# Attention, a gated layer and a rational layer in one kernel: the rational part's tile order, the place of the gated part's leftovers, and the shares of a weight conversion are changed

## The chip, the core and the metric

The program runs on one core of a Trainium2 chip. Its engines are TensorE (PE in the profile, with its weight loads as PEld), VectorE (DVE), ScalarE (ACT), GpSimd (POOL) and SyncE (SP), which here only issues transfers. The metric is the device time of one execution in microseconds, given as the median of several runs.

## The reference, cut to what matters

Local attention with a window of 32 and 32 global tokens per head, then a gated layer, then a layer with a rational function between its two products:

```python
# 4 batches x (512 local + 32 global) tokens = 2176 rows, 512 wide
out_g = softmax(q_g k_all^T / 8) v_all                       # 32 global queries see everything
out_l = softmax([q_l k_g^T, q_l k_l^T where |i-j| <= 32] / 8) [v_g, v_l]
x = concatenate([out_g, out_l])  ->  rows of 512
gate = 1 / (1 + exp(-(x @ w_gate)));  val = x @ w_val        # 512 -> 1536
x = (gate * val) @ w_out                                     # 1536 -> 512
h = x @ w_in                                                 # 512 -> 2048
P = a0 + a1 h + a2 h^2 + a3 h^3
Q = 1 + |b0| |h| + |b1| h^2
out = (P / (Q + 1e-6)) @ w_out2                              # 2048 -> 512
```

Every product is done in three: high part by high part, low by high, high by low. All inputs come as 64-bit words, of which a weight has to be rebuilt on the core (its "conversion").

## The kernel before, in words

The program is written in the order in which each engine is to run it; nothing reorders it later. A wait of one instruction therefore holds up all that is written behind it on the same engine, and on SP all transfers behind it.

**Attention** runs over 16 units (a batch and a pair of heads). Its steps are listed in `STEPS` with a number each, the place in units of progress; the list is sorted by these places and issued. `load` steps issue the transfers of q, k, v (`qn`, `kn`, `vn`, `wn`), `g_load` those of the global queries (`qgn`), which the products of line 303 (`pair<-kn,qgn`) read for every second unit. Between them stand the first weights: `w_raw` and `w_next` issue the transfer of one raw weight (`fetch`, lines 544 to 548, tile `raw`, three buffers), and `w_mag`, `w_bits`, `w_add`, `w_hi`, `w_lo` convert it: two ACTs (lines 564 and 565), two DVEs (572 and 573), a POOL addition (580), an ACT cast (602) and a POOL subtraction (610). Since there are three `raw` buffers, the transfer of weight number 5 waits until weight 1 has gone through line 573 (tile `v10gv`).

**The gated part** keeps the 2176 rows in five tiles: 0 to 3 of 512 local rows, and `GLOB` (4) of the 128 global rows. It goes through the 12 column blocks of w_gate and w_val in six pairs; in each pair tiles 0, 1 and GLOB are done: `first` (24 matmuls, gate and value, in banks of the pool `ps1`, which has three), a sigmoid on ACT (line 748, which frees the gate's bank), a product on DVE (749, which frees the value's bank), a cast and a subtraction, and `second`, two halves of 12 matmuls that DVE adds into `gacc`. Beside each pair runs a share of the conversions of later weights; `Pace` spreads them over the pair and `pace.finish()` issues what is left at its end. `AT_ONCE` says how many weights of the rational part are converted beside each pair, besides the pair's own six. A converted weight is written to DRAM (`keep`, line 594) and read back later (line 659). Behind the six pairs the sums of tiles 0 and 1 are split and sent to DRAM ("parked": lines 845 and 846, tiles `sty`), tile GLOB is turned back by `final_glob` (four transposes of line 810 into a `ps1` bank, a cast, a subtraction), and tiles 2 and 3 follow, from pair 1 on in a Strassen scheme that needs seven products of quarter size; the rest of the conversions run beside it. `back(i)` reads tile i from DRAM again, in eight transfers.

**The rational part** works in turns. A turn starts one unit: `first` (12 matmuls, line 710 to 712, or 719 to 721 for GLOB), and brings the earlier ones forward by one step each: on ACT `abs` (1150), `lin` (1153), `p3` (1161), `log` (1174), `exp` (1178), `hi` (1199); on DVE `p2` (1165), `r1` (1182), `p1` (1169), `r2` (1186), `quot` (1190); on POOL `quad` (1157) and `lo` (1211). Four turns later comes `second` (12 matmuls, lines 1240 to 1242). A GLOB unit has to be transposed on PE three turns after its start (line 1206, tile `rt`), right behind its `quot`. Within each of four groups the units come in the order `LAST_TURNS`. `rest(n)`, called at the end of turn n, issues what the gated part has left over: the last four halves of `second` (`queue`), the eight parks of tiles 2 and 3 (`parks`: a cast on ACT, line 845, and a subtraction, line 846, on DVE or POOL in turn), and `back(1)`.

Of the kernel before, what the change touches and what calls it, by code (L numbers as in the profile page):

```python
# [29 lines left out]
LN_SCALE = 2.0**-32  # L30

TILES = [(0, 512), (512, 512), (1024, 512), (1536, 512), (2048, 128)]
GLOB, LAST_TURNS = 4, (0, 4, 2, 1, 3)


def tile_of(tok):
# [76 lines left out]
    ('x_out', (397.6786, 9.48477, 15.22727, 12.74181, 508.4924, 477.88016)),  # L113
    ('w_raw', (5.02089, 6.82068, 0.49824, 10.1341)),
    ('w_next', 4, (14.0,)),
    ('w_next', 5, (14.1,)),
    ('w_next', 6, (41.0,)),
    ('w_mag', (5.27805, 7.32394, 4.37884, 25.24838)),
    ('w_bits', (5.94689, 13.87965, 5.77964, 40.08108)),
# [329 lines left out]
class Weights:  # L449
# [4 lines left out]


    EARLY, AHEAD = 4, 3
    AT_ONCE = (0, 1, 2, 1, 1, 5)
    RING2 = (4, 5, 6, 7, 0, 1, 2, 3, 8, 9, 10, 11)

    def __init__(self, tc, early, dram, ins, outs):  # L460
# [14 lines left out]
        for p, f in enumerate(range(2, NF + 1, 2)):  # L475
            m = n + self.AT_ONCE[p]
            if f < NF:
# [255 lines left out]
def gated(nc, pools, only, xpool, dram, wp, ident, xh, xl):  # L733
# [34 lines left out]
    def first(f, i):  # L768
        pg = pools.ps1.tile([128, 512], F32, tag="p1", name=f"pg{f}_{i}")
        pv = pools.ps1.tile([128, 512], F32, tag="p1", name=f"pv{f}_{i}")  # L770
        layer(nc, pg, wp, 1, f, "gate", xh[i], xl[i])
        layer(nc, pv, wp, 1, f, "val", xh[i], xl[i])
        return split(gate(pg, pv, f"{f}_{i}"), f"{f}_{i}")
# [31 lines left out]
    def final_glob():  # L805

        n = TILES[GLOB][1]
        ps = pools.ps1.tile([128, 512], F32, tag="p1", name="pty")
        for m in range(4):
            nc.tensor.transpose(ps[:, m * n : m * n + n], acc[GLOB][:, m], ident)  # L810
        yh[GLOB] = xpool.tile([128, 4, n], F32R, tag=f"xh{GLOB}", name=f"yh{GLOB}")
        yl[GLOB] = xpool.tile([128, 4, n], F32R, tag=f"xl{GLOB}", name=f"yl{GLOB}")
        src = ps.rearrange("p (m t) -> p m t", m=4)
        nc.scalar.copy(yh[GLOB], src)
        nc.vector.tensor_tensor(yl[GLOB], src, yh[GLOB].bitcast(F32), ALU.subtract)
# [54 lines left out]
    def put(i, k, x, eng):  # L870
        if not turned:
            t12h, t12l, t34h, t34l = (xpool.tile([128, 4, 512], F32R, tag=n, name=f"t{n}") for n in ("xh0", "xl0", "xh1", "xl1"))
            turned.extend([(t12h[:, 0:2], t12l[:, 0:2]), (t12h[:, 2:4], t12l[:, 2:4]),
                           (t34h[:, 0:2], t34l[:, 0:2]), (t34h[:, 2:4], t34l[:, 2:4])])
        src = held[x, k]
        h, l = (t[:, k] for t in turned[i])
        nc.scalar.copy(h, src)
        eng.tensor_tensor(l, src, h.bitcast(F32), ALU.subtract)
# [10 lines left out]
    def c1(k):  # L889
        held["a", k], held["b", k] = ztile(f"za{k}"), ztile(f"zb{k}")  # L890
        less((held["a", k], held["b", k]), at((0, 1), k), at((0, 0), k), nc.vector)
# [14 lines left out]
    def c3(k):  # L906
        held["d", k], held["e", k] = ztile(f"zd{k}"), ztile(f"ze{k}")
        less((held["d", k], held["e", k]), at((1, 1), k), at((0, 1), k), nc.gpsimd)
# [50 lines left out]
    def back(i):  # L959
        yh[i] = xpool.tile([128, 4, 512], F32R, tag=f"xh{i}", name=f"yh{i}")  # L960
        yl[i] = xpool.tile([128, 4, 512], F32R, tag=f"xl{i}", name=f"yl{i}")
        for m in range(4):
            t = wp.kept[9, i, "y", m]
            nc.sync.dma_start(yh[i][:, m].bitcast(F32), t[:, 0:512])
            nc.sync.dma_start(yl[i][:, m].bitcast(F32), t[:, 512:1024])
# [102 lines left out]
    park()  # L1068
    wp.allow(1)
    gs.append(first(1, 2))  # L1070
    final_glob()
    c1(1)
    park()
    c2(1)
# [5 lines left out]
    c4(1)  # L1080
    wp.allow(1)
    pending.pop(0)()
    put(1, 1, "b", nc.vector)
    c3(1)
    park()
# [19 lines left out]
    pace.finish()  # L1105

    def rest(n):
        for _ in range({1: 2, 2: 2}.get(n, 0)):
            queue.pop(0)()
        for _ in range({3: 4, 4: 2, 5: 2}.get(n, 0)):  # L1110
            parks.pop(0)()
        if n == 3:
            back(1)

    return yh, yl, rest

# [1 line left out]
def rational(nc, pools, rest, wp, ident, xh, xl, before, co, out):  # L1118
# [152 lines left out]
    for n in range(len(units) + 8):  # L1271
        if n == 1:
            nc.scalar.preload_act_table_set("natural_log_exp_and_others")
        for name, ahead, *args in PLAN2:
            u = n + ahead
            if name in ("second", "out") and u >= LATER:
                u -= 1
                if u < LATER:
                    continue
            if 0 <= u < len(units):  # L1280
                steps[name](u, *args)
                fs, i = units[u]
                if i == LAST_TURNS[-1] and name == "second":
                    wp.release((2, fs[0], "out", 0))
                if i == LAST_TURNS[-1] and name == "first" and fs[0] % G == G - 1:
                    for k in range(4):
                        wp.release((2, fs[0] - G + 1, "in", k))
        before(n)
        wp.pump(len(wp.loads))


@with_exitstack
def tile_kernel(ctx: ExitStack, tc, ins, out):
    nc = tc.nc
    ctx.enter_context(tc.manual_schedule())
    const = ctx.enter_context(tc.tile_pool(name="const", bufs=1))
    xpool = ctx.enter_context(tc.tile_pool(name="xpool", bufs=1))
    early = ctx.enter_context(tc.tile_pool(name="early", bufs=1))
    ident = const.tile([128, 128], F32, name="ident")
    xh = [xpool.tile([128, 4, n], F32R, tag=f"xh{i}", name=f"xh{i}") for i, (_, n) in enumerate(TILES)]  # L1300
    xl = [xpool.tile([128, 4, n], F32R, tag=f"xl{i}", name=f"xl{i}") for i, (_, n) in enumerate(TILES)]
    dram = ctx.enter_context(tc.tile_pool(name="dram", bufs=1, space=bass.MemoryType.DRAM))
    wp = Weights(tc, early, dram, {"gv": ins["w_gate_val"], "in": ins["w2_in"]},
                 {1: ins["w_out"], 2: ins["w2_out"]})

    co = const.tile([128, 8], F32, name="co")
    with ExitStack() as c:
        other = dict(w_raw=wp.fetch, w_next=lambda _, j: wp.fetch(j), w_mag=wp.magnitude, w_bits=wp.bits, w_add=wp.add, w_hi=wp.hi, w_lo=wp.lo)
        attention(c, tc, ident, xh, xl, ins, other)

    nc.sync.dma_start(co[:, 0:4], ins["a"].unsqueeze(0).to_broadcast([128, 4]))
    nc.sync.dma_start(co[:, 4:6], ins["b"].unsqueeze(0).to_broadcast([128, 2]))
    for key in wp.order[: wp.EARLY]:
        wp.keep(key, wp.have[key])
    wp.late = ctx.enter_context(tc.tile_pool(name="late", bufs=1))
    pools = Pools(ctx, tc)
    with ExitStack() as c:
        only = c.enter_context(tc.tile_pool(name="gated", bufs=1))
        yh, yl, before = gated(nc, pools, only, xpool, dram, wp, ident, xh, xl)
    rest = ctx.enter_context(tc.tile_pool(name="rest", bufs=1))  # L1320
    rational(nc, pools, rest, wp, ident, yh, yl, before, co, out)
# [70 lines left out]
```

## Time and profile before

| | |
|---|---|
| median of 3 runs | 927.42 us (927.08 to 928.08) |
| the profiled execution | 928.6 us, of which 926.8 us lie between its first and last instruction (the span) |
| attention, gated part, Strassen part, rational part | from 0, about 115, 385 and 527 us of the span on |
| TensorE's granted clock over the span | 0.99 of full speed |

The sections of the trace are given in microseconds from the span's start. In the rows of instructions the first number is the start and the second the duration; what stands in brackets at the end is how long the engine had been idle, and what ended that. A PE matmul of 512 columns is shown with 0.39 us, but in a dense row one starts every 0.227 us.

### The profile page before, as it was taken

To read this page: it belongs to the slowest core of one execution; us is meant where nothing else is said; L and a number is where in the kernel's file an instruction comes from. 1 tells how busy PE (TensorE), PEld (TensorE's weight loads), DVE (VectorE), ACT (ScalarE), POOL (GpSimd) and SP (SyncE) were. 2 spreads that over 40 slices of the span, in tenths; PEclk is the share of its full clock that TensorE was granted. 3 is DMA by queue.
4 is the path that set the end of the run, shared out by engine and by line. 5 is a ranking of instruction groups with operands and counts; after the bars stand their busy time and mean duration, and the time that the engine had idled before them with its cause. 6 is when DMAs were issued, how large, how long until landed. Compare 5 with 4: busy or idle time off the path is not lost.

```text
span 926.8 us, 13699 instructions
## 1 busy us (share of the span) xinstructions
PE 900.2 (97%) x4666; PEld 745.8 (80%) x4666; DVE 740.7 (80%) x1297; ACT 578.8 (62%) x1161; POOL 572.2 (62%) x460
## 2 busy tenths in 40 slices
PE   8989999999999998999999997999999999999998
PEld 6778888887788887888888885888888878888886
DVE  6988866989889866767776678777788898888896
ACT  6988964555454444344444376777777777777773
POOL 5776863767667573567676755445366656665664
PEclk9999999999999999999999998999999999999999
DMA  9765273767767776789999960004000410020112
GB/s 305 243 209 161 81 250 115 258 241 250 248 217 260 246 266 250 268 294 324 347 344 323 365 213 9 1 1 149 33 1 1 144 38 0 1 92 1 57 45 91
DMA packets 60804, 156.23 MB, mean 169 GB/s; under 512 B 7104, under 2 KB 9152, under 8 KB 60736
## 3 DMA queue, kind: packets, MB, share of 16 engines
q1 hardware_dynamic: 60640, 155.24, 48.3%
q8 instruction: 37, 0.61, 0.3%
q14 instruction: 31, 0.25, 0.1%
q10 hardware_dynamic: 96, 0.13, 0.1%
HBM read 103.17 MB, written 52.17 MB: 168 GB/s over the span
## 4 chain that ended last, share of the span: by engine, by line
PE 74%; DVE 12%; ACT 4%; issue 3%; POOL 3%; DMA 3%; SPq 1%; POOLq 0%; ACTq 0%; DVEq 0%
PE rp L710 6%; PE rp L712 6%; PE rp L711 6%; PE rp L1240 6%; PE rp L1242 6%; PE rp L1241 6%; PE p L830 3%; PE p L828 3%; PE p L829 3%; PE pair L260 2%; PE bank L379 2%; PE bank L361 2%; PE pb L974 1%; PE pb L976 1%; PE pb L975 1%
## 5 line engine op out<-in xcount | busy, mean ns | idle before, releaser
L1157 POOL TENSOR_TENSOR v<-v,u 128x512 f32<-128x512 f32 x68 | 90.0, 1323 | 121.5 <-ACT v L1153 121.5
L1211 POOL TENSOR_TENSOR rgl<-t,rgh 128x512 fp32r<-128x512 f32 x64 | 89.3, 1395 | 36.9 <-POOL v L1157 20.9
L1165 DVE TENSOR_TENSOR t<-rp,t 128x512 f32<-128x512 f32 x68 | 46.9, 689 | 49.3 <-ACT t L1161 48.0
L1150 ACT ACTIVATE u<-rp 128x512 f32<-128x512 f32 x68 | 40.6, 597 | 72.3 <-PE rp L712 69.3
L294 POOL TENSOR_TENSOR p<-p,r 128x448 f32<-128x448 f32 x64 | 58.9, 944 | 33.5 <-DVE r L289 20.6
L1186 DVE SCALAR_TENSOR_TENSOR v<-v,u 128x512 f32<-128x512 f32 x68 | 75.2, 1106 | 0.0
L756 ACT CAST gh<-t 128x512 fp32r<-128x512 f32 x38 | 23.6, 620 | 82.1 <-DVE t L749 73.0
L1190 DVE SCALAR_TENSOR_TENSOR t<-t,co,v 128x512 f32<-128x512 f32 x68 | 70.1, 1031 | 2.4
L279 ACT ACTIVATE p<-p,mx 128x224 f32<-128x224 f32 x128 | 60.2, 480 | 6.2 <-DVE mx L271 6.2
L842 DVE TENSOR_TENSOR gacc<-p,gacc 128x512 f32<-128x512 f32 x80 | 51.6, 682 | 11.2 <-PE p L830 11.0
L1182 DVE SCALAR_TENSOR_TENSOR v<-v,u 128x512 f32<-128x512 f32 x68 | 57.4, 844 | 1.1 <-ACT u L1178 1.1
L761 DVE TENSOR_TENSOR gl<-t,gh 128x512 fp32r<-128x512 f32 x38 | 35.8, 941 | 27.8 <-ACT gh L756 27.8
L1153 ACT ACTIVATE v<-u,co 128x512 f32<-128x512 f32 x68 | 55.6, 817 | 2.3
L1161 ACT ACTIVATE t<-rp,co 128x512 f32<-128x512 f32 x68 | 51.8, 762 | 2.5 <-POOL rgl L1211 2.5
L1174 ACT ACTIVATE u<-v,co 128x512 f32<-128x512 f32 x68 | 49.2, 724 | 6.3 <-POOL v L1157 6.1
L1169 DVE SCALAR_TENSOR_TENSOR t<-t,co,rp 128x512 f32<-128x512 f32 x68 | 50.3, 739 | 0.0
L1178 ACT ACTIVATE u<-u,co 128x512 f32<-128x512 f32 x68 | 48.5, 714 | 2.3 <-DVE t L1165 2.2
L271 DVE CUSTOM_DVE_ANT_0 p<-pair,masks 128x224 f32<-128x224 f32 x128 | 42.2, 384 | 6.7 <-DMA masks<-in_masks 6.3
L1199 ACT CAST rgh<-t 128x512 fp32r<-128x512 f32 x64 | 39.0, 609 | 12.5 <-DVE t L1190 12.5
L1265 POOL TENSOR_TENSOR racc<-ev,racc 128x512 f32<-128x512 f32 x22 | 37.9, 1743 | 0.0
L749 DVE TENSOR_TENSOR t<-pv,t 128x512 f32<-128x512 f32 x28 | 19.2, 686 | 22.8 <-PE pv L712 14.0
L260 PE MATMUL pair<-kn,qn 64*128 64x224 f32 x256 | 30.1, 367 | 1.3 <-DMA qn<-in_q_l 0.5
(1344 smaller groups left out, 3180.4 us busy)
## 6 DMA issues: line engine op xcount, KB each, us to landing
raw1gv<-in_w_gate_val SPq DMA_DIRECT2D x24, 512.0 KB, 4.1
raw2in<-in_w_in SPq DMA_DIRECT2D x16, 512.0 KB, 5.2
raw2out<-in_w_out SPq DMA_DIRECT2D x16, 512.0 KB, 4.6
kn<-in_k_l SPq DMA_DIRECT2D x15, 448.0 KB, 5.2
raw1out<-in_w_out SPq DMA_DIRECT2D x12, 512.0 KB, 4.3
vn<-in_v_l SPq DMA_DIRECT2D x16, 256.0 KB, 3.6
out<-racc SPq DMA_DIRECT2D x16, 256.0 KB, 2.0
qn<-in_q_l SPq DMA_DIRECT2D x15, 256.0 KB, 4.4
```

Of the source, the lines that this page charges most:

```text
L279: nc.scalar.activation(p, p, AF.Exp, bias=s["mx", half][:, n : n + 1], scale=-1.0, accum_out=s["sm", half][:, n, 0:1])
L294: nc.gpsimd.tensor_tensor(p, p, r, ALU.mult)
L710: nc.tensor.matmul(ps, wh, mh[:, k], start=k == 0, stop=False)
L711: nc.tensor.matmul(ps, wh, ml[:, k], start=False, stop=False)
L712: nc.tensor.matmul(ps, wl, mh[:, k], start=False, stop=k == 3)
L1157: nc.gpsimd.tensor_tensor(s["v"], s["v"], s["u"], ALU.mult)
L1182: nc.vector.scalar_tensor_tensor(s["v"], s["v"], Q_CONST, s["u"], ALU.add, ALU.mult)
L1186: nc.vector.scalar_tensor_tensor(s["v"], s["v"], 2.0, s["u"], ALU.subtract, ALU.mult)
L1190: nc.vector.scalar_tensor_tensor(s["t1"], s["t1"], a0, s["v"], ALU.add, ALU.mult)
L1211: nc.gpsimd.tensor_tensor(s["gl"], s["t1"], s["gh"].bitcast(F32), ALU.subtract)
L1240: nc.tensor.matmul(ps, gh[:, w], wh, start=k == 0, stop=False)
L1241: nc.tensor.matmul(ps, gh[:, w], wl, start=False, stop=False)
```

## The change

Six places are changed. The order of the rational turns becomes tile 0, tile 1, GLOB, tile 2, tile 3. `back(1)` moves from the end of turn 3 to turn 0; the last four halves of `second` are spread over turns 1 to 3 (two, one, one) where turns 1 and 2 had two each; the eight parks come one a turn in turns 3 to 10, where turn 3 had four and turns 4 and 5 two each; and all this now stands right behind the turn's `first` and not at its end. `AT_ONCE` gives pair 0 one weight of the rational part and takes one from pair 2 and one from pair 5, so that each of pairs 0 to 4 has seven conversions and pair 5 four; the conversion taken from pair 5 runs beside the Strassen part. `final_glob` moves behind the first half of the next `second`. The transfer of raw weight 5 moves from place 14.1 to 15.0 of the attention's list.

```diff
-GLOB, LAST_TURNS = 4, (0, 4, 2, 1, 3)
+GLOB, LAST_TURNS = 4, (0, 1, 4, 2, 3)
...
-    ('w_next', 5, (14.1,)),
+    ('w_next', 5, (15.0,)),
...
-    AT_ONCE = (0, 1, 2, 1, 1, 5)
+    AT_ONCE = (1, 1, 1, 1, 1, 4)
...
     gs.append(first(1, 2))
-    final_glob()
     c1(1)
...
     pending.pop(0)()
+    final_glob()
     put(1, 1, "b", nc.vector)
...
     def rest(n):
-        for _ in range({1: 2, 2: 2}.get(n, 0)):
+
+        for _ in range({1: 2, 2: 1, 3: 1}.get(n, 0)):
             queue.pop(0)()
-        for _ in range({3: 4, 4: 2, 5: 2}.get(n, 0)):
+        if n == 0:
+            back(1)
+        if 3 <= n < 11:
             parks.pop(0)()
-        if n == 3:
-            back(1)
...
                 steps[name](u, *args)
+                if name == "first":
+                    before(n)
...
-        before(n)
         wp.pump(len(wp.loads))
```

**SP in attention.** These are transfers on SP's queue around unit 10, before (`raw1out` is a raw weight, `qgn` the global queries that line 303 reads):

```order
L232 DMA qn_103<-in_q_l 128x512
L548 DMA raw1out_921<-in_w_out 128x1024
L548 DMA raw1out_929<-in_w_out 128x1024
L232 DMA kn_102<-in_k_l 128x896
L240 DMA qgn_110<-in_q_g 128x128
L232 DMA vn_106<-in_v_l 128x512
```

and the same stretch now:

```order
L548 DMA raw1out_921<-in_w_out 128x1024
L232 DMA kn_102<-in_k_l 128x896
L240 DMA qgn_110<-in_q_g 128x128
L232 DMA vn_106<-in_v_l 128x512
L232 DMA qn_104<-in_q_l 128x512
L232 DMA vn_108<-in_v_l 128x512
L228 DMA wn_128<-in_w_l 96x512
L548 DMA raw1out_1019<-in_w_out 128x1024
```

The second raw weight has gone behind the keys, the global queries and four more transfers.

**ACT at the end of gated pair 2.** `v20in` and `q20in` are a conversion's first step, `st6s` and `w16out` later steps of others, `t_1<-pg_1` is the sigmoid of the pair's last `first`. Before:

```order
L602 CAST w17gv_0_2726<-v17gv_2639 128x2x256
L564 ACTIVATE v20in_2754<-raw2in_2652 128x512
L565 ACTIVATE q20in_2755<-raw2in_2652 128x512
L639 CAST st6s_2758<-v16gv_2478 128x2x256
L639 CAST st6s_2765<-v16gv_2536 128x2x256
L602 CAST w16out_0_2772<-v16out_2688 128x512
L756 CAST gh_glob<-pt_2774 128x256
L748 ACTIVATE t_1_2807<-pg_1_2781 128x512
```

and now:

```order
L602 CAST w17gv_0_2756<-v17gv_2653 128x2x256
L756 CAST gh_glob<-pt_2763 128x256
L748 ACTIVATE t_1_2796<-pg_1_2770 128x512
L756 CAST gh_1_2799<-t_1_2796 128x512
L564 ACTIVATE v20in_2808<-raw2in_2699 128x512
L565 ACTIVATE q20in_2809<-raw2in_2699 128x512
L639 CAST st6s_2812<-v16gv_2492 128x2x256
```

One conversion is gone from the place, and the steps `st6s` and `w16out` stand behind the sigmoid.

**DVE in the rational turns 3 to 6.** `yl<-gacc` is a park, lines 1165 to 1190 (1166 to 1191 now) are the rational steps. Before, from turn 3 on:

```order
L1165 TENSOR_TENSOR t_5843<-rp_5826,t_5843 128x512
L1182 SCALAR_TENSOR_TENSOR v_5772<-v_5772,u_5770 128x512
L846 TENSOR_TENSOR yl_5734<-gacc_4171,yh_5733 128x512 x2
L1169 SCALAR_TENSOR_TENSOR t_5843<-t_5843,co,rp_5826 128x512
L1186 SCALAR_TENSOR_TENSOR v_5772<-v_5772,u_5770 128x512
L1190 SCALAR_TENSOR_TENSOR t_5774<-t_5774,co,v_5772 128x512
L1165 TENSOR_TENSOR t_5892<-rp_5875,t_5892 128x512
L1182 SCALAR_TENSOR_TENSOR v_5841<-v_5841,u_5839 128x512
L846 TENSOR_TENSOR yl_5798<-gacc_4325,yh_5797 128x512
```

and now, from turn 4 to turn 6:

```order
L846 TENSOR_TENSOR yl_5734<-gacc_4148,yh_5733 128x512
L1166 TENSOR_TENSOR t_5888<-rp_5869,t_5888 128x512
L1183 SCALAR_TENSOR_TENSOR v_5849<-v_5849,u_5847 128x512
L1170 SCALAR_TENSOR_TENSOR t_5888<-t_5888,co,rp_5869 128x512
L1187 SCALAR_TENSOR_TENSOR v_5849<-v_5849,u_5847 128x512
L1191 SCALAR_TENSOR_TENSOR t_5851<-t_5851,co,v_5849 128x512
L1166 TENSOR_TENSOR t_5937<-rp_5918,t_5937 128x512
L1183 SCALAR_TENSOR_TENSOR v_5886<-v_5886,u_5884 128x512
L1170 SCALAR_TENSOR_TENSOR t_5937<-t_5937,co,rp_5918 128x512
L1187 SCALAR_TENSOR_TENSOR v_5886<-v_5886,u_5884 128x512
L1191 SCALAR_TENSOR_TENSOR t_5888<-t_5888,co,v_5886 128x512
L846 TENSOR_TENSOR yl_5734<-gacc_4148,yh_5733 128x512
```

DVE has a park in turns 4, 6, 8 and 10, where it had two in turn 3 and one each in turns 4 and 5.

## Rows read from the trace of the kernel before

**Rows 1.** The page, part 1: busy time of each engine, share, instructions.

```profile
PE 900.2 (97%) x4666; PEld 745.8 (80%) x4666; DVE 740.7 (80%) x1297; ACT 578.8 (62%) x1161; POOL 572.2 (62%) x460
```

**Rows 2.** PE's own waits over the span: total us, times, longest us.

```profile
PE rt L1206 <- DVE t L1190: 7.8, 2, 6.1
PE pg L710 <- ACT t L748: 3.8, 2, 2.8
PE pair L303 <- DMA qgn<-in_q_g: 3.1, 1, 3.1
```

**Rows 3.** Attention unit pairs: length; PE, PEld, DVE, ACT, POOL busy; PEclk; DMA; GB/s.

```profile
43.10:56.00 12.90, 12.90 (x144) 11.39 (x143) 12.11 (x63) 12.26 (x48) 8.33 (x10) 1.00 0.56 176
56.00:73.80 17.80, 14.74 (x143) 12.61 (x143) 13.49 (x63) 11.96 (x47) 10.17 (x10) 0.90 0.63 212
```

**Rows 4.** SP's queue in order of time, 57.7 to 64.5 us.

```profile
58.19 5.47 SPq L548 DMA_DIRECT2D raw1out<-in_w_out  x2
...
64.17 0.43 SPq L240 DMA_DIRECT2D qgn<-in_q_g  x1
```

**Rows 5.** SP's own waits, the one of line 548 for weight 1.

```profile
SPq L548 <- DVE v10gv L573: 4.7, 1, 4.7
```

**Rows 6.** What the DMA engines moved, 55 to 70 us, in 40 slices.

```profile
GB/s 322 284 246 300 339 358 225 279 229 266 255 261 386 418 392 453 229 109 33 11 0 0 0 0 98 131 262 350 317 336 373 392 356 239 309 355 361 371 404 410
```

**Rows 7.** Gated pairs, from one GLOB product to the next; columns as in rows 3.

```profile
132.82:170.00 37.18, 37.18 (x178) 31.21 (x177) 25.94 (x38) 16.96 (x31) 18.09 (x14) 1.00 0.51 172
...
207.18:248.58 41.40, 39.07 (x177) 32.27 (x176) 38.18 (x49) 21.04 (x39) 29.05 (x21) 0.96 0.69 237
248.58:286.98 38.40, 37.45 (x177) 31.26 (x176) 32.52 (x43) 18.75 (x34) 25.46 (x19) 1.00 0.73 251
286.98:324.15 37.17, 37.17 (x177) 31.20 (x176) 32.83 (x41) 18.01 (x33) 24.27 (x18) 1.00 0.72 247
```

**Rows 8.** ACT in order of time behind the last gated pair.

```profile
354.56 0.66 ACT L564 ACTIVATE v24in<-raw2in 128x512 f32<-128x512 f32 x1 [2.65 <-POOL st22out L610]
...
364.11 0.59 ACT L748 ACTIVATE t<-pg 128x512 f32<-128x512 f32 x1
```

**Rows 9.** Stretches around three stalls, a steady turn, four transposes; columns as in rows 3.

```profile
361.34:369.17 7.83, 5.01 (x18) 3.82 (x17) 7.14 (x11) 3.77 (x7) 2.39 (x2) 0.79 0.66 239
554.84:578.47 23.63, 16.83 (x65) 12.86 (x64) 21.18 (x23) 14.54 (x24) 14.29 (x9) 0.86 0.08 30
755.75:763.58 7.83, 6.13 (x29) 4.82 (x28) 7.63 (x10) 5.01 (x8) 2.91 (x2) 1.00 0.00 0
742.35:747.79 5.44, 5.44 (x25) 4.50 (x24) 5.19 (x8) 4.79 (x9) 3.38 (x3) 1.00 0.28 99
668.24:668.60 0.36, 0.36 (x6) 0.36 (x4) 0.36 (x2) 0.20 (x1) 0.30 (x1) 1.00 0.00 0
```

**Rows 10.** A DVE turn with a park and one without; columns as in rows 3.

```profile
560.30:566.79 6.49, 5.75 (x26) 4.42 (x25) 5.93 (x7) 4.98 (x8) 4.68 (x3) 1.00 0.00 0
755.62:760.20 4.58, 3.01 (x14) 2.16 (x12) 4.54 (x7) 3.82 (x6) 2.91 (x2) 1.00 0.00 0
```

**Rows 11.** DVE's park in the first of these turns.

```profile
562.11 1.36 DVE L846 TENSOR_TENSOR yl<-gacc,yh 128x512 fp32r<-128x512 f32 x1 [0.53 <-ACT yh L845]
```

**Rows 12.** The page, part 5: DVE's additions into the gated sums.

```profile
L842 DVE TENSOR_TENSOR gacc<-p,gacc 128x512 f32<-128x512 f32 x80 | 51.6, 682 | 11.2 <-PE p L830 11.0
```

**Rows 13.** SP's queue ahead of the rational part.

```profile
535.62 0.32 SPq L594 DMA_DIRECT2D k215out<-st215out  x1
```

**Rows 14.** The page, part 6: the transfers of one back(i), median us to landing.

```profile
yh<-k91y SPq DMA_DIRECT2D x4, 256.0 KB, 6.2
```

**Rows 15.** A Strassen weight: its transfer on SP, its first use on PE.

```profile
442.70 0.32 SPq L659 DMA_DIRECT2D w18g<-k18g  x1
...
467.78 0.39 PE L974 MATMUL pa<-xh,w18g 128*128 128x512 f32 x1
```

**Rows 16.** The Strassen part's DMA load; columns as in rows 3.

```profile
500.00:520.00 20.00, 20.00 (x90) 16.57 (x89) 13.11 (x18) 8.94 (x17) 13.02 (x11) 1.00 1.00 370
```

## The prediction

> **What bounds the kernel now.** I read the engines' busy times first: PE is busy for 900.2 us of a span of 926.8, all others for 80% or less [rows 1]. So the kernel is as long as PE's work and PE's losses, and an edit is worth what it does to a stretch in which PE loses time. Next come PE's own waits: three carry nearly all, rt behind DVE (7.8 us in two waits, the longest 6.1), pg behind the ACT sigmoid (3.8, the longest 2.8) and pair of line 303 behind qgn (3.1) [rows 2]. A wait isn't the whole loss: where PE has stood still, the granted clock of the stretch is 0.79 to 0.96 and not 1.00 [rows 3, 7, 9], so part of the work behind ran at the lower of its two levels (1.2 GHz, against 2.4). I therefore price a stall by the length of the stretch around it, less that of the same work without one. These windows are all that the sum needs.
>
> **The change part by part.**
>
> *The later raw weight.* Two attention units take 12.90 us, and with line 303's wait among them 17.80 [rows 3]: 4.90 lost, 3.1 of it waiting and 1.8 of clock and restart. What is late? qgn is issued at 64.17, because SP has stood from 58.19 on at two raw transfers, 5.47 us for both [rows 4], of which 4.7 is one wait for weight 1's pass through line 573 [rows 5]. The order shows the second of the two gone from ahead of qgn. The 4.7 and one issue, (5.47 - 4.7) / 2 = 0.4, then no longer stand there: qgn goes out about 5.1 earlier, where 3.1 would do. Slack 2.0, so the whole 4.90 should go. The raw transfer itself now stands seven transfers later, when what it waited for (63.7, the end of its wait) is over, so nothing new queues behind it; its weight is used in the gated part, at about 115, and has time. **-4.9.**
>
> Here the Trainium skill speaks against the edit: "DMA: Bandwidth & Descriptors", section "Issuing engines are not separate DMA queues", says that all transfers run in the end on the same 16 DMA engines, whichever engine starts them, and that issuing is usually small beside the transfer. By that the bytes ahead of qgn would count and not its place on SP, and removing one raw transfer (512 KB) would save its bytes alone. The row on what moved decides first: four slices of 0 GB/s, of 0.375 us each, and two of 33 and 11 lie ahead of the 98 with which the flow begins again, so for about 2 us the engines had nothing to do [rows 6]. It wasn't bytes, but SP, that held qgn. By the bytes the edit would be worth 512 KB at some 270 GB/s (the mean of the slices around), 1.9 us in place of 4.9.
>
> *The shares of the conversions.* From one GLOB product to the next a gated pair takes 37.17 or 37.18 us where nothing stalls, and 41.40 and 38.40 around pair 2, the one with eight conversions [rows 7]: 4.23 + 1.23. The order shows what stands ahead of the last sigmoid of that pair on ACT: an eighth conversion's two passes, two casts st6s and one of w16out. Now they stand behind it or are gone. A pair with seven runs at 37.17 with DVE at 32.83 and POOL at 24.27; the pair without a seventh has DVE at 25.94 [rows 7], so pair 0 takes one more conversion (some 6.9 us of DVE) within its 37.18. The 1.23 is the less sure part, since it falls in a pair of seven; I count it as what was left over from the pair before. **-5.5** (bounds: 4.2 and 5.5). The conversion that pair 5 gives away runs beside the Strassen part, where PE is full, DVE at 13.1, ACT at 8.9 and POOL at 13.0 of 20 us, but the DMA engines at 1.00 [rows 16]. Its cover is the distance of a weight's transfer (442.70) from its first use (467.78), 25.1 us [rows 15], against 6.2 for transfers of 256 KB [rows 14]. I cost it at nothing.
>
> *final_glob and one conversion less in pair 5.* 361.34 to 369.17 is 7.83 long at a clock of 0.79; its work is half a steady turn (5.44 / 2 = 2.72) and four transposes (0.36) [rows 9]. So 4.75 is lost, of which 2.8 is the wait for a sigmoid [rows 2] that runs at 364.11, on an ACT that had stood 2.65 us at a conversion's first pass, for POOL [rows 8]. That conversion is the one moved away, and final_glob's bank of ps1 is taken half a second later, so the bank that first wants is no longer shared by three. Either alone is worth about the 2.65, so the sigmoid would be there 2.65 earlier by the first alone, against a wait of 2.8. **-4.75** (bounds: 2.65 and 4.75).
>
> *The rational turns.* 554.84 to 578.47 is 23.63 at a clock of 0.86; its work is five halves of a turn and four transposes, 13.60 + 0.36 [rows 9]. So 9.67 is lost: the transposes come three turns after GLOB's start, directly behind DVE's quot, and DVE is behind because of the parks (6.1 of wait [rows 2]; a park turn takes DVE 6.49, one without 4.58 [rows 10], a steady turn of PE 5.44 [rows 9]). GLOB now starts four turns later. At the next GLOB unit, 755.75 to 763.58, 7.83 is spent on 5.44 + 0.36 [rows 9]: 2.03 lost, because it follows by three turns a turn that has no second; now seven turns lie between them, in which DVE (4.58 a turn) catches up. **-9.7 and -2.0.**
>
> What may come back: the new rt. PE wants it at first(4) + 7 turns, which is 554.84 - 5.44 + 7 x 5.44 = 587.5. DVE has from there a park in turns 4, 6 and 8 (the order), so three turns of at most 6.49 and three of 4.58, 33.2 against PE's 32.6: 0.6 behind; the two copies that empty the first sums, at the 0.68 of an addition of this size [rows 12], make 2.0. Upper bound: 2.0 and as much again for clock and restart as at the sigmoid (4.75 - 2.8), 4.0. Lower bound: nothing, because the 6.49 holds 0.53 of waiting for ACT's cast [rows 11] and lay beside a park on POOL as well, of which each turn now has only one or the other. I take 1.2, nearer to the lower, since three times 0.53 already takes 1.6 of the 2.0 away. **+1.2.**
>
> *Costed at nothing.* back(1), eight transfers, stands behind SP's last write of a converted weight (535.62) [rows 13]; at 0.32 to 0.5 each it is issued by 539.9 and, at 6.2 [rows 14], there by 546.1. Tile 1 is first wanted by turn 4, at 549.4: slack 3.3. Without it every us late would be a us of PE. The weights behind it on SP belong to the second group, some 17 turns on. The spread of the last halves (two, one, one) adds none. Parks now start in turn 3 and end in turn 10; nothing reads tiles 2 and 3 before turn 9, and park eight belongs to tile 3, read from turn 13.
>
> **The sum.** 4.90 + 5.46 + 4.75 + 9.67 + 2.03 = 26.81 off, 1.2 on: 25.6 less. The profiled execution took 928.6 (span 926.8 and 1.8 around it), 1.2 above the median of 927.4. On the median: 927.4 - 25.6 = 901.8, say 902.0. PE's 900.2 is no floor against this: it counts the slowed matmuls at their slow length.
>
> **The rivals.**
>
> *One stall stays or moves* (0.18). For it: three waits have slack of 2 to 3 us only (qgn, back(1), the sigmoid), and the new rt has none. Against it: each has its late instruction named. Price 4 to 5 (a stall's 2.8 to 3.1 and its restart 1.8 to 1.95): 902.0 + 4.5 = 906.5, between 905 and 911.
>
> *The bytes count, not SP's place* (0.08). The mechanism of the qgn edit without its place in the queue: 1.9 in place of 4.9, 905.0. The slices of 0 GB/s speak against it. It is the rule of the Trainium skill named above ("DMA: Bandwidth & Descriptors", "Issuing engines are not separate DMA queues").
>
> *Two or more stalls stay* (0.10). All five prices are differences of windows; where two causes were taken for one, as in pair 3's 1.23, they stay. From 902 + 9 = 911 (two of the middle ones) to 925.
>
> *Nothing comes of it* (0.03). Each stall gives way to another of its size, since ACT and DVE work as much as before: 925.5 to 929.3, which is within 0.2% (1.9 us, about what a measurement of this kernel can tell from no change).
>
> *Slower, by the Strassen weights* (0.05). One more conversion goes through DMA engines that are at 1.00 already [rows 16]: 512 KB raw and 512 KB back, 2.8 us at 370 GB/s, and each later weight moves back. From the point at which the 25.1 of cover [rows 15] is used up, each of some ten blocks waits: at least 1 us and 1.8 of restart, 28 us, and the time is 902 + 28 = 930 or more. The cover is nine times the 2.8, which speaks against it.
>
> *All five go* (the likeliest, 0.56): 898.5 to 905, from rt at nothing (901.8 - 1.2 = 900.6) and two us of error in the windows, to rt at its upper bound (901.8 - 1.2 + 4.0 = 904.6).
>
> **How the numbers follow.** 902.0 is the likeliest's. The likeliest, the bytes' rival and the moved stall hold 0.82 and lie between 898.5 and 911: that is the range. Faster by over 0.2%: 0.56 + 0.18 + 0.08 + 0.10 = 0.92; within 0.2%: 0.03; slower: 0.05.
>
> **What would show it.** Right: no wait of line 303 for qgn and no slice without traffic at 62 us; all gated pairs at 37.2; no sigmoid in PE's waits above 1 us; the first rt wait at 2 us or less, near 560 to 590; the third GLOB unit without one; the clock at 1.00 in all these stretches. Wrong: qgn issued before 60 and PE waiting nevertheless (bytes); a wait of PE in pair 0 or 1, which the moved conversions would have brought; a wait for yh at line 710 in turn 4 (back(1)); waits for w tiles in the Strassen part.

## The result and the profile after

The changed kernel takes 902.34 us (median of 4 runs, 901.85 to 902.87) against 927.75 (927.08 to 929.05) beside it: 25.4 less, a ratio of 0.9725 with an interval of 0.9708 to 0.9741. 902.0 was predicted, 25.6 less. The execution profiled took 902.8 with a span of 900.8. In the runs below, the first executions of both_early and strassen_28, in which they were also profiled, were disturbed (5,148 and 996 us) and are left out: what is told of the two rests on their other three, and for strassen_28 on a second profile.

The page of the changed kernel, parts 1 and 2: busy time of each engine, and TensorE's granted clock in 40 slices.

```profile
PE 892.7 (99%) x4666; PEld 742.1 (82%) x4666; DVE 752.8 (84%) x1297; ACT 578.2 (64%) x1161; POOL 578.1 (64%) x460
...
PEclk9999999999999999999999999999999999999999
```

Its PE waits: total us, times, longest us.

```profile
PE bank L361 <- POOL p L294: 1.3, 3, 0.8
PE bank L222 <- DVE still L199: 1.1, 1, 1.1
PE rp L1241 <- DVE racc L1262: 0.6, 1, 0.6
...
PE rt L1207 <- DVE t L1191: 0.2, 1, 0.2
```

The three waits of [rows 2] are gone; 0.2 is left of rt. PE is busy for 7.5 us less with the same 4666 matmuls, because what had run at the lower clock runs at the full one (1.00 in all windows below, against 0.94 to 0.99); the rest was idle time. Where the time went is read from windows between the same places: the two attention units around qgn, all gated pairs from the first GLOB product to the last, from there to the first rational product, and the rational part. Columns as in [rows 3]; of before:

```profile
52.44:83.13 30.69, 27.63 (x287) 23.99 (x284) 25.14 (x122) 24.20 (x90) 19.52 (x23) 0.94 0.62 203
132.94:324.27 191.33, 188.06 (x883) 157.15 (x881) 162.35 (x205) 93.89 (x172) 122.23 (x87) 0.99 0.67 230
324.27:527.62 203.35, 200.43 (x889) 165.40 (x888) 144.21 (x197) 89.85 (x160) 130.64 (x98) 0.99 0.87 309
527.62:922.48 394.86, 385.78 (x1696) 317.77 (x1695) 323.18 (x399) 284.91 (x452) 228.41 (x164) 0.99 0.15 53
```

and of the changed kernel, with one pair (0 to 1) and the Strassen window as well:

```profile
52.72:78.79 26.07, 25.97 (x286) 22.64 (x283) 24.96 (x123) 24.20 (x91) 19.48 (x23) 1.00 0.73 239
128.62:165.80 37.18, 37.18 (x179) 31.21 (x177) 28.74 (x39) 17.62 (x32) 19.98 (x15) 1.00 0.62 213
128.62:314.50 185.88, 185.88 (x882) 156.01 (x881) 161.07 (x205) 91.78 (x169) 120.91 (x86) 1.00 0.69 237
314.50:512.74 198.24, 198.24 (x890) 164.29 (x889) 152.58 (x196) 90.68 (x161) 132.51 (x98) 1.00 0.88 314
500.00:520.00 20.00, 20.00 (x90) 16.53 (x90) 12.97 (x20) 8.76 (x17) 14.37 (x11) 1.00 1.00 365
512.74:896.53 383.79, 383.00 (x1697) 316.55 (x1695) 328.33 (x400) 284.89 (x452) 233.73 (x164) 1.00 0.16 56
```

| stretch | less by, us | predicted |
|---|---|---|
| start to the first GLOB product (132.94 to 128.62) | 4.3 | 4.9 |
| gated pairs | 5.45 | 5.46 |
| end of pair 5, Strassen part | 5.1 | 4.75 |
| rational part | 11.1 | 9.67 + 2.03 - 1.2 = 10.5 |
| sum | 25.95 | 25.6 |

Where a conversion was added, pair 0 has grown from 25.94 to 28.74 of DVE and still takes 37.18 [rows 7]; the Strassen part is at 1.00 on DMA as before [rows 16], and PE is busy through all its 198.24.

One sign came out otherwise than the prediction asked. It wanted no slice without traffic at 62 us. What the DMA engines move in the changed kernel, 55 to 70 us, in the same 40 slices of 0.375 us as [rows 6]:

```profile
GB/s 295 268 322 290 339 306 259 287 337 284 219 205 325 393 422 382 391 442 370 422 287 148 29 21 0 0 0 0 0 147 218 366 344 361 262 229 202 224 295 317
```

There are still five slices of 0, now from 64.0 us on. SP issues qgn at 59.36 and then waits 5.2 for PE (line 388) before its next transfer, yet no wait of PE is shown between 52 and 80 us. So slices of 0 don't by themselves show that PE loses, and the prediction's reading of [rows 6] needs the experiment early_bits below.

### The profile page after: what moved, and what is told of

The parts are those of the page before. It is cut to its first block, busy times and chain, and to the rows that moved or that the text cites. A ratio compares the mean times of both kernels' runs of the same rounds, so it can differ in the third digit from the quotient of the medians.

```text
span 900.8 us, 13701 instructions
## 1 busy us (share of the span) xinstructions
PE 892.7 (99%) x4666; PEld 742.1 (82%) x4666; DVE 752.8 (84%) x1297; ACT 578.2 (64%) x1161; POOL 578.1 (64%) x460
## 4 chain that ended last, share of the span: by engine, by line
PE 86%; DVE 9%; ACT 2%; POOL 1%; issue 1%; POOLq 0%; DVEq 0%; ACTq 0%
PE rp L1241 6%; PE rp L1242 6%; PE rp L1243 6%; PE rp L712 5%; PE rp L710 5%; PE rp L711 5%; PE p L828 4%; PE p L830 4%; PE p L829 4%; PE pg L710 3%; PE pg L711 3%; PE pg L712 3%; PE pv L710 3%; PE pv L711 3%; PE pv L712 3%; PE pair L260 2%
## 5 line engine op out<-in xcount | busy, mean ns | idle before, releaser
L1158 POOL TENSOR_TENSOR v<-v,u 128x512 f32<-128x512 f32 x68 | 93.6, 1376 | 105.2 <-ACT v L1154 103.0
L1191 DVE SCALAR_TENSOR_TENSOR t<-t,co,v 128x512 f32<-128x512 f32 x68 | 72.9, 1072 | 2.4
L1187 DVE SCALAR_TENSOR_TENSOR v<-v,u 128x512 f32<-128x512 f32 x68 | 74.1, 1089 | 0.0
L279 ACT ACTIVATE p<-p,mx 128x224 f32<-128x224 f32 x128 | 60.2, 480 | 6.5 <-DVE mx L271 6.5
L1183 DVE SCALAR_TENSOR_TENSOR v<-v,u 128x512 f32<-128x512 f32 x68 | 61.7, 908 | 1.1 <-ACT u L1179 1.1
```

The lines of the kernel that those rows point to most:

```text
L279: nc.scalar.activation(p, p, AF.Exp, bias=s["mx", half][:, n : n + 1], scale=-1.0, accum_out=s["sm", half][:, n, 0:1])
L1158: nc.gpsimd.tensor_tensor(s["v"], s["v"], s["u"], ALU.mult)
L1183: nc.vector.scalar_tensor_tensor(s["v"], s["v"], Q_CONST, s["u"], ALU.add, ALU.mult)
L1187: nc.vector.scalar_tensor_tensor(s["v"], s["v"], 2.0, s["u"], ALU.subtract, ALU.mult)
L1191: nc.vector.scalar_tensor_tensor(s["t1"], s["t1"], a0, s["v"], ALU.add, ALU.mult)
```

## The experiments

Each kernel is the changed one with one edit or two taken back or added, but for early_bits, which is an edit of before. The times beside them of the kernel before were 928.6 to 928.9, about 1 above those beside the changed kernel, so the windows tell more exactly than the medians.

**What held the global queries.** undo_raw:

```diff
-    ('w_next', 5, (15.0,)),
+    ('w_next', 5, (14.1,)),
```

> The changed kernel with the transfer of raw weight 5 back at place 14.1. By SP's place: SP stands about 4.7 us at that transfer again, line 303 waits about 3.1 for qgn, two attention units take 17.8 again, and the time is 4.3 to 4.9 above the changed kernel's 902.3: 906.6 to 907.2. By the bytes (the transfer's 512 KB at some 270 GB/s): 1.9 above, 904.2.

907.19 (905.73 to 908.78), 4.85 above; ratio to before 0.9773 (0.9758 to 0.9787). Line 303 waits 3.2 for qgn again. The bytes' 1.9 is below even the fastest of its four runs (905.73, 3.4 above). early_bits leaves the transfer where before had it and lets weight 1 go through lines 572 and 573 sooner:

```diff
-    ('w_bits', (5.94689, 13.87965, 5.77964, 40.08108)),
+    ('w_bits', (5.94689, 12.0, 5.77964, 40.08108)),
```

> The kernel before, with weight 1's pass through lines 572 and 573 at place 12.0 of the attention's list in place of 13.88; both raw transfers stay ahead of qgn. By SP's place: the wait of 4.7 at line 548 goes, qgn is issued before 60 and the wait of line 303 goes, 4.3 to 4.9 below before: 922.9 to 923.5. By the bytes: those of both raw transfers still run ahead of qgn, so that at most 3.0 are gained: 924.8 or more, with a wait for qgn left at line 303.

924.25 (923.74 to 924.42), 0.9955 (0.994 to 0.997) of before. SP's queue in early_bits, and the product that waits for qgn:

```profile
58.06 0.84 SPq L548 DMA_DIRECT2D raw1out<-in_w_out  x2
58.95 0.43 SPq L232 DMA_DIRECT2D kn<-in_k_l  x1
59.42 0.57 SPq L240 DMA_DIRECT2D qgn<-in_q_g  x1
...
65.42 1.17 PE L303 MATMUL pair<-kn,qgn 128*64 128x512 f32 x8
```

Both raw transfers are still ahead of qgn, with all their bytes, yet the two take SP 0.84 and not 5.47 [rows 4], qgn goes out at 59.42, and no wait for qgn is left at line 303. 52.32 to 78.62 takes 26.30, 4.39 below before's 30.69. So SP's place it was, not the bytes. The Trainium skill's "DMA: Bandwidth & Descriptors", section "Issuing engines are not separate DMA queues", calls issuing usually small beside the transfer. That agrees with the 0.42 of an issue here. What held qgn up was not an issue but SP's wait of 4.7 ahead of one [rows 5].

**Which conversion stalls the pairs.** pair2_eight:

```diff
-    AT_ONCE = (1, 1, 1, 1, 1, 4)
+    AT_ONCE = (0, 1, 2, 1, 1, 4)
```

> The changed kernel with six, seven, eight, seven, seven and four conversions beside the six pairs, so that one goes from pair 0 back to pair 2. If the eighth conversion makes both long stretches: pair 2 to 3 at 41.4, pair 3 to 4 at 38.4, 5.5 above the changed kernel's 902.3: 907.8. If the 1.2 of pair 3 was its own: 4.2 above, 906.5. If pair 2 stalled for another reason that the change took away: 902.3.

908.31 (907.49 to 909.3), 6.0 above; 0.9785 (0.977 to 0.9799). Its pairs 2 to 3 and 3 to 4, and PE's only wait in each:

```profile
203.38:244.62 41.24, 38.89 (x178) 32.17 (x177) 38.02 (x49) 20.92 (x39) 28.97 (x21) 0.96 0.67 239
244.62:283.04 38.42, 37.49 (x178) 31.26 (x177) 32.55 (x43) 18.72 (x34) 25.51 (x19) 1.00 0.69 251
...
PE pv L710 <- ACT t L748: 2.3, 1, 2.3
PE pg L710 <- ACT t L748: 0.9, 1, 0.9
```

Both long stretches of [rows 7] come back from one conversion in one pair: 4.07 and 1.25, 5.3 in all. The 1.2 in pair 3 is therefore a leftover of pair 2, as counted. The waits are for the sigmoid, and before has the same two in its two long stretches, 2.3 and 0.9. Which of the eighth conversion's steps on ACT makes the sigmoid late wasn't tried.

**final_glob or the conversion beside pair 5.** undo_glob puts final_glob back, pair5_five the conversion:

```diff
     gs.append(first(1, 2))
+    final_glob()
     c1(1)
...
     pending.pop(0)()
-    final_glob()
     put(1, 1, "b", nc.vector)
```

```diff
-    AT_ONCE = (1, 1, 1, 1, 1, 4)
+    AT_ONCE = (1, 1, 1, 1, 1, 5)
```

> The changed kernel with final_glob back ahead of the first half of second, pair 5 still with four conversions. If the conversion alone held ACT: no sigmoid wait, 902.3. If the bank that final_glob takes is a cause of its own: a wait at line 710 of up to 2.8 and up to 4.75 above, 904.5 to 907.

> The changed kernel with five conversions beside pair 5 in place of four, final_glob still at its new place. If the later place of final_glob alone is enough: 902.3. If ACT, held up at the conversion's first pass, is what PE waits for: the wait for the sigmoid near 350 to 361 comes back with 2 to 2.8 us and the time is 2 to 4.75 above: 904.5 to 907.

undo_glob: 903.27 (902.82 to 903.8), 0.9724 (0.9709 to 0.9738) of before, as the changed kernel. pair5_five: 907.75 (907.42 to 908.65), 0.9773 (0.9759 to 0.9788). The stretch from the last GLOB product to the rational part, first in undo_glob:

```profile
315.01:513.67 198.66, 198.65 (x889) 164.20 (x888) 152.92 (x195) 90.68 (x161) 132.40 (x98) 1.00 0.87 313
```

then in pair5_five, with ACT at the place of [rows 8] and two of PE's waits:

```profile
314.91:517.68 202.77, 199.30 (x890) 164.04 (x888) 145.45 (x198) 89.81 (x160) 130.92 (x98) 1.00 0.87 309
...
345.77 0.67 ACT L564 ACTIVATE v24in<-raw2in 128x512 f32<-128x512 f32 x1 [2.65 <-POOL st22out L610]
346.34 0.65 ACT L565 ACTIVATE q24in<-raw2in 128x512 uint32<-128x512 uint32 x1
346.90 0.58 ACT L748 ACTIVATE t<-pg 128x512 f32<-128x512 f32 x1
...
PE pa L974 <- DVE yl L815: 2.2, 1, 2.2
PE pv L710 <- ACT t L748: 1.1, 1, 1.1
```

With before (203.35: both old) and the changed kernel (198.24: both new) these are the four cases. Taking the conversion away is worth 203.35 - 198.66 = 4.7 without the move of final_glob, the move 203.35 - 202.77 = 0.6 without the other, both 5.1. pair5_five also shows why the move alone is worth so little: the sigmoid behind v24in still comes late (346.90, where the changed kernel has it at 340.78), and with it the next one, for which PE waits 1.1; and the bank that final_glob now takes later is still held, by DVE's subtraction of line 815, when the first Strassen product wants one. The stall changes its place.

**GLOB's place, or the parks.** glob_early takes back GLOB's place alone (tile 1 stays ahead of tile 2, which before had the other way round), undo_parks the spread of the parks alone, both_early both:

```diff
-GLOB, LAST_TURNS = 4, (0, 1, 4, 2, 3)
+GLOB, LAST_TURNS = 4, (0, 4, 1, 2, 3)
```

```diff
-        if 3 <= n < 11:
+        for _ in range({3: 4, 4: 2, 5: 2}.get(n, 0)):
             parks.pop(0)()
```

> The changed kernel with the rational turns in the order tile 0, GLOB, tile 1, 2, 3, parks still one a turn. If GLOB's later place is what takes rt's wait away: a wait of 2 to 4 us for rt at its turn 7 with a restart of about 1.9, and the 2.0 of the third group back: 906 to 910. If the spread of the parks does it: no wait at turn 7 and the 2.0 alone: 904.3.

> The changed kernel with the eight parks as before (four in turn 3, two each in turns 4 and 5), GLOB still behind tiles 0 and 1. The run with GLOB early has shown that the spread of the parks alone takes the wait for rt at turn 7 away. If GLOB's later place alone does so too (each suffices): no wait for rt, 902.3 to 903.3. If DVE's lag of two parks lasts until turn 11, or the bunch of parks holds up another step (a second that waits for POOL's rgl): a wait of 2 to 6 us, 905 to 911.

> The changed kernel with GLOB second in the rational turns and with the parks as before, four in turn 3 and two each in turns 4 and 5; what rest issues still stands right behind first. If each of the two edits was enough by itself, the wait for rt at turn 7 is back with some 6 us and the rational part is 9 to 11 us longer than that of the changed kernel (383.8): 911 to 913. If it was the place in the turn that did it: the wait at the third group alone, 904.

glob_early: 903.98 (903.69 to 904.13), 0.9737 (0.9721 to 0.9754); undo_parks: 904.04 (903.71 to 905.11), 0.9735 (0.9718 to 0.9751); both_early: 909.5 to 911.1 in three runs, the middle one 909.8, 0.9804 (0.9783 to 0.9826). The transposes of the four groups in glob_early, and below them its rational part:

```profile
550.39 0.66 PE L1207 MATMUL rt<-ident,t 128*128 128x128 f32 x4
...
735.53 0.66 PE L1207 MATMUL rt<-ident,t 128*128 128x128 f32 x4 [1.71 <-DVE t L1191]
...
512.16:897.70 385.54, 383.25 (x1697) 316.51 (x1695) 325.28 (x400) 284.81 (x452) 230.94 (x164) 1.00 0.16 56
```

and the first group's in undo_parks:

```profile
574.12 0.66 PE L1207 MATMUL rt<-ident,t 128*128 128x128 f32 x4 [1.02 <-DVE t L1191]
...
512.70:897.73 385.03, 383.30 (x1696) 316.59 (x1695) 327.94 (x400) 284.62 (x452) 231.84 (x164) 1.00 0.16 56
```

With GLOB early and the parks spread, the first rt doesn't wait; with GLOB late and the parks bunched it waits 1.0. With both as they were, 909.8 - 902.3 = 7.5 come back. So each edit by itself takes away nearly all of the first stall. Singly they are worth little: GLOB's place 385.54 - 383.79 = 1.75, the third group's wait (1.7), and the spread 385.03 - 383.79 = 1.24, the 1.0 left at the first; the other 4.5 of the 7.5 go by either. 7.5 is less than the 9 to 11 that were expected of both_early, and isn't all of the rational part's 11.1. About 3.6 is left, which can only come from what both_early keeps of the change: rest's place right behind first, the new turns of the last halves and of back(1), and tile 1 ahead of tile 2. Which of these it is, no run shows. both_early has no profile that shows its waits, so this split goes by the times alone.

**When back(1) is issued.** late_back moves it to turn 3 again; late_back_queue also issues the last halves two and two:

```diff
-        if n == 0:
-            back(1)
         if 3 <= n < 11:
             parks.pop(0)()
+        if n == 3:
+            back(1)
```

```diff
-        for _ in range({1: 2, 2: 1, 3: 1}.get(n, 0)):
+        for _ in range({1: 2, 2: 2}.get(n, 0)):
```

> The changed kernel with back(1) at the end of turn 3 as before, where tile 1 is wanted by turn 4. By the cover counted in the prediction (transfers of 6.2 us and eight issues, against the end of one turn without second): first(4) waits 4 to 7 us for yh and about 2 of restart come on top: 908 to 912. If transfers from an idle set of DMA engines land in less than half that time: under 905.

> The changed kernel with back(1) in turn 3 and the last halves of second two and two, so that on SP the two transfers of w24in stand ahead of back(1) and wait for PE's last half, as before. Issued then some 18 us behind the rational part's start instead of 9, the last of eight lands about 8 us too late for first(4), the first about 3 to 5: a wait for yh of 3 to 8 us and about 2 of restart, 907 to 912. If less of tile 1 is needed at first(4) than counted, or it lands faster: 902.3 to 904.

late_back: 903.4 (902.72 to 903.82), 0.9724 (0.971 to 0.9739), no change. late_back_queue: 908.87 (908.1 to 909.6), 0.9788 (0.9768 to 0.9809). SP's queue in late_back, first and last of back(1)'s eight:

```profile
521.64 0.32 SPq L594 DMA_DIRECT2D k215out<-st215out  x1
522.01 0.42 SPq L964 DMA_DIRECT2D yh<-k91y  x1
...
525.71 0.61 SPq L965 DMA_DIRECT2D yl<-k91y  x1
533.24 1.68 SPq L659 DMA_DIRECT2D w24in<-k24in  x2
```

and in late_back_queue, with PE's first(4):

```profile
522.45 0.32 SPq L594 DMA_DIRECT2D k215out<-st215out  x1
531.32 1.68 SPq L659 DMA_DIRECT2D w24in<-k24in  x2
533.05 0.42 SPq L964 DMA_DIRECT2D yh<-k91y  x1
...
538.95 0.77 PE L710 MATMUL rp<-yh,w20in 128*128 128x512 f32 x1 [3.58 <-DVE v L1183]
```

The time expected of late_back if the transfers land fast came out, but not for that reason. SP goes through its list as fast as its waits allow: written in turn 3, the eight transfers still go out at 522, since nothing ahead of them on SP waits any longer. It is the two transfers of w24in that wait, for PE's last half (line 830), and which side of them back(1) stands on depends on the turn of that half. Behind them it goes out 11 us later and PE waits 3.6 (the view names DVE, but line 710 reads yh, whose first transfer was issued 5.9 before); with the restart, 389.80 in place of 383.8 for the rational part.

**More conversions beside the Strassen part.** strassen_28 takes one from each of pairs 0 to 4; strassen_28_again is the same kernel, profiled once more:

```diff
-    AT_ONCE = (1, 1, 1, 1, 1, 4)
+    AT_ONCE = (0, 0, 0, 0, 0, 4)
```

> The changed kernel with six conversions beside each of pairs 0 to 4, so that 28 in place of 23 run beside the Strassen part. By the cover counted in the prediction (25.1 us against 2.8 us of transfers for each): five are 14 us, no weight is late, and it stays at 902.3 to 904. If the Strassen part has no room on DMA, ACT or POOL: waits for w tiles on PE or conversions left over behind its end, 5 us for each, 907 to 930.

> The same kernel as strassen_28, for its profile: its timed runs were 12 to 13 us above the changed kernel. If the DMA engines are the limit: waits on PE for w tiles (lines 974 and on) spread over the Strassen part, with DMA at 1.00, about 1 to 2 us each. If the conversions run out of time on their engines: no wait in the Strassen part's blocks, but one or two longer ones at its end and at the rational part's first weights, 8 to 12 us in all.

914.0 to 915.4 in three runs, the middle one 914.9, 0.9854 (0.9833 to 0.9875); 915.63 in the last. That is 12.5 for five conversions, and neither theory had its cause. The waits of PE in strassen_28_again, the stretch to the rational part, DVE's queue in one Strassen block, and the product that waits in it:

```profile
PE pb L974 <- DVE w L989: 3.9, 7, 1.0
...
315.49:522.83 207.34, 201.50 (x889) 163.51 (x888) 150.13 (x209) 98.42 (x174) 145.28 (x107) 1.00 0.90 325
...
439.10 0.81 DVE L572 TENSOR_SCALAR v27out<-v27out 128x512 uint32<-128x512 uint32 x1 [1.59 <-ACT v27out L564]
439.95 0.69 DVE L573 SCALAR_TENSOR_TENSOR v27out<-raw2out,v27out 128x512 uint32<-128x512 uint32 x1
440.56 0.68 DVE L989 TENSOR_TENSOR w<-pb,s 128x512 f32<-128x512 f32 x1
...
441.29 0.50 PE L974 MATMUL pb<-txh,w16s 128*128 128x512 f32 x1 [0.43 <-DVE w L989]
```

No weight's transfer is waited for. What is late is DVE: a conversion's step, which itself waits 1.59 for ACT, stands ahead of the addition that empties the bank pb, and PE waits 0.3 to 1.0 for that bank in seven of the blocks; in each, DVE has stood 0.7 to 1.6 for ACT at such a step just before. That accounts for 3.9 of the stretch's 9.1 (207.34 - 198.24). Three more waits of PE in it make 1.8 (0.7 and 0.6 for steps of weight w111out's conversion, 0.5 for ACT's copy of a Strassen sum); another 3.3 is PE's own busy time, 201.50 against 198.24 for as many matmuls. Why the steps come late on ACT isn't traced further, nor are the 3.4 that lie outside this stretch.

## Why the prediction was right, point by point

- **The raw weight: right, a little too large.** 4.9 was forecast, 4.3 came up to the first GLOB product, 4.6 in the window around qgn (30.69 to 26.07), and early_bits shows the cause, SP's place. The bytes' rival is out. (The transfer stands six places later in the order shown, not seven; nothing hangs on it.)
- **The conversions: right** to 0.1, with the 1.2 of pair 3 put where it belongs. Two readings on the way were off. "Three carry nearly all" leaves out the wait behind this very stall, pv for the sigmoid (2.3), which the prediction priced by its window all the same. And the conversion added to pair 0 took 2.8 of DVE (25.94 to 28.74), not "some 6.9".
- **Pair 5: the sum right, its split wrong.** "Either alone is worth about the 2.65" fell: 4.7 for the conversion, 0.6 for final_glob. It was a cause and a side show. Of the 5.1, 4.7 lies ahead of the first Strassen product (382.81 - 324.27 before, 368.36 - 314.50 now), beside the 4.75 forecast.
- **The rational turns: the size right (11.7 of stalls, 11.1 gained), the cause half told.** The text let the first stall go because "GLOB now starts four turns later". The runs show that the spread of the parks takes it away as well without that, that both together are worth 7.5 of the 11.1, and that some 3.6 came from elsewhere in the change. The new rt was counted at 1.2; it waits 0.2, at 572.95, that is 60.2 behind the rational part's start, where the sum had 587.5 - 527.6 = 59.9. DVE kept pace, but not by the turns that were counted. From one p2 (line 1166) to the sixth after it, 541.74 to 574.51, DVE took 32.8 with three parks and the two copies, where the sum had 33.2 + 1.4 = 34.6. A turn with a park took 5.2 to 5.4 and not 6.49, one without 5.1 to 5.4 (the copies left out) and not 4.58; the two errors partly cancel. One reason was named by the bounds: a park no longer waits for ACT's cast (no idle time is shown ahead of the two in the last section).
- **back(1) at nothing: right, but only half of why.** The prediction looked at what stands ahead of back(1) on SP and didn't name w24in, which in before had stood ahead of it (issued at 545.51, back(1) from 547.25 on). Writing back(1) in turn 0 keeps it ahead of w24in, and so does the spread of the last halves (late_back); with both taken back it costs 6. So "the spread of the last halves adds none" holds only while back(1) stands in turn 0, and that case (turn 0 without the spread) is argued from SP's order, not run.
- **The Strassen part.** One conversion more beside the Strassen part is free, as forecast. Five more cost 12.5, less than the 28 of that rival and by another way: as far as it is resolved, DVE's queue and not the DMA engines, since no wait for a weight's transfer is shown.
- **The clock.** "Where PE has stood still" the clock isn't always down: the prediction's own rows have 1.00 in pair 3 [rows 7] and around the third GLOB unit [rows 9], where the waits are short (0.9 and 1.7). The sum isn't touched by this, since it goes by windows.
- **The sum** held because its terms were read as lengths of windows, which don't depend on which of two edits removes a stall. That it came within 0.4 is in part luck: the raw weight gave 0.6 less than forecast, pair 5 and the rational part 0.4 and 0.6 more. The causes had to be found by the runs.

## What to carry to other kernels

Where one engine bounds the kernel, price each of its stalls as the window's length less that of the same work elsewhere, restart and clock included, and add them up: here five such differences made 26.8, and the windows afterwards showed 25.95, 3% less. Don't read from such a sum which edit did it: undo them one by one and also together, since two edits can each be enough. On an engine that only issues, the turn in which a step is written means little; what counts is which waiting instruction stands ahead of it (late_back and late_back_queue).

## What the runs showed of the hardware

One DVE instruction of the same shape takes 0.68 or 1.79 us, and the rows put it down to POOL. DVE's parks in turns 4 and 6 of the changed kernel, and POOL's work around them:

```profile
541.14 0.68 DVE L846 TENSOR_TENSOR yl<-gacc,yh 128x512 fp32r<-128x512 f32 x1
550.80 1.79 DVE L846 TENSOR_TENSOR yl<-gacc,yh 128x512 fp32r<-128x512 f32 x1
552.51 0.68 DVE L1166 TENSOR_TENSOR t<-rp,t 128x512 f32<-128x512 f32 x1
```

```profile
541.95 1.30 POOL L1212 TENSOR_TENSOR rgl<-t,rgh 128x512 fp32r<-128x512 f32 x1 [1.28 <-ACT rgh L1200]
...
550.40 1.65 POOL L1158 TENSOR_TENSOR v<-v,u 128x512 f32<-128x512 f32 x1 [0.85 <-ACT v L1154]
552.19 1.57 POOL L1212 TENSOR_TENSOR rgl<-t,rgh 128x512 fp32r<-128x512 f32 x1
```

The first park ends before POOL begins at 541.95; the second runs beside POOL's 550.40 to 552.05 and lasts 1.1 longer. The addition at 552.51 runs beside POOL too and isn't slowed: one of its inputs is a bank of products. The rest of the trace has the same: of DVE's four parks one took 0.68 and three 1.77 to 1.79, while all 68 additions of line 1166, most of them beside POOL, took 0.68 to 0.69. The Trainium skill has this on the page "SBUF — State Buffer", section "SBUF: two separate sides": an exclusive lock on a port pair that both engines share, which a VectorE instruction takes only where it reads two SBUF inputs (or runs in a two-port mode). The three rows agree with it.
